# Weighing the kept sums of two experts on VectorE, and adding them by DMA, in a fused attention and mixture-of-experts kernel

## The chip, the cores and the metric

The kernel runs on one core of a Trainium2 chip. The metric is the time of one execution on the device, in microseconds (us), as the median of several runs. Lower is better. Engines are called PE (TensorE, the matrix engine), DVE (VectorE), ACT (ScalarE), POOL (GpSimd) and SP (SyncE, which here does nothing but issue transfers).

## The reference, cut to what matters

An attention block turns `q`, `k`, `v` into `x`, 4352 tokens of 128 features. Then a mixture of eight experts, with weights `P` for each token and expert that come from a balancing iteration, makes the output:

```
def _moe_ref(x, w_gate, w1, w2):            # x 4352 x 128, w1 8 x 128 x 1024, w2 8 x 1024 x 128
    P = np.exp(x @ w_gate - max)
    for _ in range(8):                      # rows, then columns, scaled to equal sums
        ...
    out = np.zeros((N, D))
    for e in range(8):
        ye = np.maximum(x @ w1[e], 0.0) @ w2[e]
        out += P[:, e:e + 1] * ye
    return out
```

Every expert is applied to every token. A weight `P[:, e]` is positive, so it may be multiplied onto a token's `x` ahead of the two products and the relu between them, or onto the expert's output behind them. All of it is float32.

## The kernel before

The features lie along the 128 partitions and the tokens along the columns (`xT`, 128 x 4352). `P` depends on all tokens, so the weights are ready only some way into the kernel. They lie in DRAM as `pT`, one row for each expert, and a row is read into SBUF as a broadcast over the partitions (`weights_of`, L788).

**Groups and items.** Work is cut into groups of tokens (`groups`, L713) and, within a group, into its experts; a group and an expert are an item. Groups 0 to 7 are done ahead of the weights: they apply expert 0 to all tokens and expert 1 to the first 1280. Their results stay in SBUF without a weight, as `kept[0]` (128 x 4352) and `kept[1]` (128 x 1280). From group 8 (`PLAIN`) on, `x` is multiplied by the weights first, so the products of all experts of a group can be summed in PSUM. Groups 8 to 12 have 768 tokens each, as three parts of 256 (`NT3`), starting at tokens 1280, 512, 2048, 2816 and 3584; they run experts 1 to 7, the one at 512 experts 2 to 7. The last group is the 512 tokens from 0, with experts 2 to 7.

**The middle stage.** These weighted groups of three parts are run by `middle()` (L1258). An item is two blocks; a block makes 128x384 first products (`x` times `w1`, PE, L1275), their relus and copies on ACT (L1301 to L1307), sums of them on DVE (L1312, L1177), and second products (the sums times sums of `w2`, PE, L1492). Both matrix products are done with fewer multiplications than the plain form has, which is what the sums on DVE are for: ten a block on L1177, four on L1312. The order of instructions on PE, DVE and ACT is written out by hand: `add(at, do)` enters a step at a due time, in a period of `PERIOD` = 8.83 us per block, and the steps are issued in order of these times. The due times only set the order; the engines run as soon as their semaphores allow. POOL and SP get their instructions in the order of the program too (`keep_in_program_order`). DVE, ACT, POOL and SP each run their queue in order, so an instruction that waits holds up all behind it.

**Spare slots.** Work that is not tied to a place, such as bringing the output together, goes into a list, `later`. `at_ease()` is called three times for each block (`EASE`) and issues one piece of `later` each time; pieces of `soon` are issued at once at the next call. `at_leisure(do)` puts a piece into `later` by way of `soon`.

**The input of an item.** `fetch_weights` (L815) loads the 768 weights of an item as `px`, on SP. `weigh_half` (L825, L832) multiplies `xT` by them on DVE, in two halves of 384 columns. The second half is wanted with a minus sign, so `negate` (L818, L823) makes a negated copy of that half of `xT` on ACT once per group. `copy_half` copies both halves on ACT, and `join_halves` (L843, L848) adds across halves and partitions with four accumulating DMAs on POOL's queue. The joined tiles `xe` and `de` feed PE.

**The kept sums.** `weigh_kept` (L853) brings the results of experts 0 and 1 into a weighted group. For each kept expert, it loads the weights of the group's tokens (`pb`) and multiplies `kept` by them, in pieces of 128x256, on POOL (`weigh`, L797): three pieces for each group of three parts, six for the group at 512 (where expert 1 is kept as well), four for the last group. Where expert 1 is kept, an accumulating DMA (`plus`) adds `kept[1]` to `kept[0]`; for the last group a subtraction on half of the partitions follows on POOL (`less`, L873). These steps are entered 5, 8.7, 12.4 and 16.1 us behind the start of an item near the beginning of the group (the third and later ones in `PLAIN`).

**The output of a group.** When a group's sums in PSUM are complete, `evacuate` and `part_of_twenty` (L990) copy them to SBUF and bring the four banks together in `y` (three parts of 128x256), with some twenty additions and subtractions on DVE (L999) through the spare slots. The last of these are three additions of the weighted `kept[0]` (L1039, L1040). Then `put` (L882) transposes each part on DVE (`yt`, L884) and stores it from SP (L1050), four or eight transfers for each.

Of the kernel before, what the change touches and what calls it, by code (L numbers as in the profile page):

```python
# [10 lines left out]
F32 = mybir.dt.float32  # L11
U32 = mybir.dt.uint32
Act = mybir.ActivationFunctionType
Alu = mybir.AluOpType
# [36 lines left out]
def kernel(  # L51
# [12 lines left out]
    nc = tc.nc  # L64
    P = nc.NUM_PARTITIONS
# [49 lines left out]
    own = consts.tile([P, H], F32, name="own")  # L115
# [9 lines left out]
    xT = big.tile([P, N + 2 * 32], F32, name="xT")  # L125
# [11 lines left out]
    pT = dram.tile([E, N], F32, name="pT")  # L137
# [14 lines left out]
    for i in range(2):  # L152
        t = wk.tile([P, H + 1, NT + 1, D], F32, name=f"v{i}", bufs=1)
# [3 lines left out]
    loaded, pools = {}, []  # L157
# [551 lines left out]
    NT3 = 256  # L709
# [6 lines left out]
    PLAIN = len(groups)  # L716
# [8 lines left out]
    kept = [keep.tile([P, N], F32, name="kept0"), keep.tile([P, 1280], F32, name="kept1")]  # L725
    items = [(g, e) for g, group in enumerate(groups) for e in group[3]]
# [59 lines left out]
        store_four(items[j][1], loaded_w[j][2])  # L786

    def weights_of(e, lo, n, tag):  # L788
        if tag == "pb":
            pb = spare[:, 6 * NT3 + 2 * HALF:9 * NT3 + 2 * HALF][:, 0:n]  # L790
        else:
            pb = pools[0].tile([P, 3 * NT3], F32, tag=tag, name=tag, bufs=3)[:, 0:n]
        tc.keep_in_program_order(nc.sync.dma_start(out=pb, in_=pT[e:e + 1, lo:lo + n].to_broadcast([P, n])))
        return pb

    def weigh(out, x, pb):
        tc.keep_in_program_order(nc.gpsimd.tensor_tensor(out, x, pb, op=Alu.mult))  # L797
# [12 lines left out]

    HALF = 3 * NT3 // 2
    spare = hb[:, 25 * NT3:]
    weights, turned_off = {}, {}

    def fetch_weights(j):  # L815
        weights[j] = weights_of(items[j][1], groups[items[j][0]][0], 3 * NT3, "px")

    def negate(g):  # L818

        lo = groups[g][0]  # L820
        c = 6 * NT3 + HALF * (g % 2)
        x = turned_off[g] = spare[:, c:c + HALF]
        nc.scalar.activation(out=x, in_=xT[:, lo + HALF:lo + 2 * HALF], func=Act.Copy, scale=-1.0)  # L823

    def weigh_half(j, i, engine):  # L825

        g = items[j][0]
        lo = groups[g][0]
        if i == 0:
            sources[j] = [pools[0].tile([P, 2, HALF], F32, tag="xe", name="xe", bufs=3)]  # L830
        x = turned_off[g] if i else xT[:, lo:lo + HALF]
        ins = engine.tensor_tensor(sources[j][0][:, i], x, weights[j][:, HALF * i:HALF * (i + 1)], op=Alu.mult)  # L832
        if engine is nc.gpsimd:
            tc.keep_in_program_order(ins)

    def copy_half(j, i):

# [12 lines left out]
    first_weighted = next(j for j, (g, e) in enumerate(items) if g == PLAIN)  # L850
    first_new = first_weighted + 2

    def weigh_kept(g, i):  # L853

        lo, n, t, es, _ = groups[g]
        ys = [kept[e][:, lo:lo + n * t] for e in range(es[0])]
        if i < len(ys):
            pb = []

            def piece(c):  # L860
                if not c:
                    pb.append(weights_of(i, lo, n * t, "pb"))
                sl = slice(c, c + NT3)
                weigh(ys[i][:, sl], ys[i][:, sl], pb[0][:, sl])

            return [lambda c=c: piece(c) for c in range(0, n * t, NT3)]

        def plus(y):
            tc.keep_in_program_order(nc.gpsimd.dma_start(out=ys[0], in_=y, accum_op=Alu.add))

        def less():
            k1, k2 = ys[0][upper, 0:n], ys[0][upper, n:2 * n]
            tc.keep_in_program_order(nc.gpsimd.tensor_tensor(k1, k1, k2, op=Alu.subtract))  # L873

        return [lambda y=y: plus(y) for y in ys[1:]] + [less] * (t == 2)

    def at_leisure(do):

        soon.append(lambda: later.append(do))
# [110 lines left out]
    def part_of_twenty(g, k):  # L990
# [7 lines left out]
        def do(out, a, b, off=False):  # L998
            at_leisure(lambda: nc.vector.tensor_tensor(out, a, b, op=Alu.subtract if off else Alu.add))  # L999

        if k == 0:
            own["y"] = pools[0].tile([P, 3, NT3], F32, tag="y", name="y")
            do(own["y"][:, 0], own[0][:, 0], own[0][:, 1])
        y = own["y"]
        if k == 1:
            do(y[:, 1], own[1][:, 0], own[0][:, 0], True)
        elif k == 2:
            do(y[upper, 2], own[2][upper, 0], own[0][upper, 0], True)
            do(y[lower, 2], own[2][lower, 0], own[0][lower, 1], True)
            do(y[lower, 2], y[lower, 2], own[2][lower, 1], True)  # L1010
            do(y[lower, 1], y[lower, 1], own[1][lower, 1], True)
        if all(i in own for i in range(4)):
            e0, e1, e2, e3 = (own[i] for i in range(4))
            t, c = (room(a).rearrange("p (s n) -> p s n", s=2) for a in "rx")
# [21 lines left out]
            do(y[:, 0], y[:, 0], c[:, 0])  # L1036
            do(y[upper, 2], y[upper, 2], t[upper, 1], True)
            do(y[lower, 2], y[lower, 2], d[lower], True)
            for i in range(3):  # L1039
                do(y[:, i], y[:, i], kept[0][:, lo + NT3 * i:lo + NT3 * (i + 1)])  # L1040
            for i in range(3):
                at_leisure(lambda i=i: put(y[:, i], lo + NT3 * i, NT3, (nc.sync,)))

# [214 lines left out]
    def middle():  # L1258
# [4 lines left out]
        def add(at_, do, *a):  # L1263
            jobs.append((at_, len(jobs), lambda: do(*a)))
# [98 lines left out]
        def at_ease():  # L1363
            while soon:
                soon.pop(0)()
            if later:
                later.pop(0)()

        for n, k in enumerate([ks[0] - 1] + ks, -1):
            if k == ks[-1] or items[blocks[k][0]][0] != items[blocks[k + 1][0]][0]:  # L1370
# [2 lines left out]
        for n, k in enumerate(ks):  # L1373
# [5 lines left out]
            if q == 0:  # L1379
# [17 lines left out]
                        add(t + at_, lambda: sums_ahead[j + 1].pop(0)())  # L1397
                late = 2 if g == PLAIN else 0
                if 1 + late <= es.index(e) <= es[0] + 1 + late:
                    for i, do in enumerate(weigh_kept(g, es.index(e) - 1 - late)):  # L1400
                        add(t + 5 + 3.7 * i, do)
                if g == len(groups) - 2 and 3 <= es.index(e) <= 5:
                    for i, do in enumerate(weigh_kept(len(groups) - 1, es.index(e) - 3)):
                        add(t + 5 + 3.7 * i, do)
            ahead = j + 2 + q
            if new_of(ahead):
                if q:
                    add(t + WEIGH - 9, fetch_weights, ahead)
                    if items[ahead - 1][0] != items[ahead][0]:
                        add(t + WEIGH, negate, items[ahead][0])  # L1410
                add(t + WEIGH, weigh_half, ahead, 1 - q, nc.vector)
                add(t + 13.69, copy_half, ahead, 1 - q)
                if not q:
                    add(t + WEIGH + 1, join_halves, ahead)
# [29 lines left out]
        for i, at_ in enumerate((10, 20.13, t + 15.43, t + 20.13, 2 * t + 15.43, 2 * t + 18, 2 * t + 28, 2 * t + 26,  # L1444
                                 3 * t + 20)):
            add(at_, lambda i=i: own[i]())
        add(WEIGH - 0.6, weigh_half, first_new + 2, 0, nc.vector)
        add(WEIGH - 0.2, copy_half, first_new + 2, 0)
        def begin_two(k):
            ready[k] = two(k)  # L1450
# [57 lines left out]
    def beside(j, c):  # L1508
# [17 lines left out]
        if new_of(j + 1) or new_of(j + 2):  # L1526
            for do, *a in PREPARE.get(c if new_of(j + 1) else c - 16, ()):
# [1 line left out]

    pieces, BESIDE = [], {}  # L1530

    PREPARE = {-14: ((fetch_weights, first_new),), -9: ((weigh_half, first_new, 0, nc.vector),),
               -8: ((negate, PLAIN), (copy_half, first_new, 0)), -7: ((weigh_half, first_new, 1, nc.vector),),
               -6: ((copy_half, first_new, 1),), -5: ((join_halves, first_new),),
               0: ((fetch_weights, first_new + 1), (raw_second, first_new, "ws"), (first_weights, first_new)),
               4: ((weigh_half, first_new + 1, 0, nc.vector),), 5: ((weigh_half, first_new + 1, 1, nc.vector),),
               6: ((copy_half, first_new + 1, 0),), 7: ((copy_half, first_new + 1, 1),),
               8: ((join_halves, first_new + 1),)}

# [191 lines left out]
```

## Time and profile before

| what | value |
|---|---|
| time, median of 3 runs | 892.82 us (892.56 to 892.99) |
| the profiled execution's own time, and its span | 892.21 us, 890.4 us |
| PE busy | 880.1 us (99% of the span) |
| DVE busy | 788.3 us (89%), 1595 instructions |
| ACT busy | 561.7 us (63%) |
| POOL busy | 180.9 us (20%), 242 instructions |
| mean granted TensorE clock | 0.999 |
| HBM traffic over the span | 167 GB/s |

The span is the stretch that the profiler's records cover; the execution's own time has 1.8 us around it. "Busy" counts an engine while it has an instruction under way. PE works as row tiles of 64x64, two or more at a time, so a busy PE may still have one of its tiles idle. In the views below, "L1177 DVE ... hb<-hb" is the instruction of line 1177 on DVE that writes tile `hb` and reads tile `hb`; "SPq" and "POOLq" are queues that issue transfers. In a row of the groups of instructions, the count is followed by the busy time in us and the mean of one in ns, then the idle time of the engine ahead of them and what ended it. A row of the timeline has its start, the stretch that it covers, and the number of instructions that it holds. A row of windows has the stretch and its length, and the busy time and number of instructions of PE, PEld (weight loads), DVE, ACT and POOL, then the granted clock, the DMA engines' busy share and GB/s.

### The profile page before, as it was taken

Reading aid. Unit: us, or ns where it says so; the run is one execution under the profiler, and the core shown is the slowest. Engines: PE = TensorE matmul, PEld = TensorE weight load, DVE = VectorE, ACT = ScalarE, POOL = GpSimd, SP = SyncE. Lnnn points to the kernel's source line nnn. Section 1 sums busy time; section 2 is a strip of 40 time slices with the busy share of each in tenths; the row PEclk is TensorE's granted clock in tenths of the full one; section 3 lists DMA queues with packets and bytes.
Section 4 is the critical chain, followed back from the end, with each engine's and each line's share of the span. In section 5 each row is a group of like instructions: output and inputs, shape, how many; then the busy total and the mean of one; then the engine's idle time right before and its main releaser. Section 6 shows DMA issues by size and latency. Waiting matters only on the chain.

```text
span 890.4 us, 28221 instructions
## 1 busy us (share of the span) xinstructions
PE 880.1 (99%) x11586; PEld 615.3 (69%) x11586; DVE 788.3 (89%) x1595; ACT 561.7 (63%) x1288; POOL 180.9 (20%) x242
## 2 busy tenths in 40 slices
PE   8999999999999999999999999999999999999997
PEld 6777544555677777676777777777777786666665
DVE  7678788889799999999999998999989999987865
ACT  3355477666577676676767666766667676655543
POOL 3121123012133213321222211321122213100000
PEclk9999999999999999999999999999999999999999
DMA  9996359658989777767776687567676775750340
GB/s 257 304 282 228 95 106 215 165 151 184 292 249 237 233 209 239 205 183 187 215 238 160 179 213 227 170 186 211 197 194 186 233 210 152 173 176 28 116 103 13
DMA packets 92721, 169.13 MB, mean 190 GB/s; under 512 B 28704, under 2 KB 65008, under 8 KB 87744
## 3 DMA queue, kind: packets, MB, share of 16 engines
q1 hardware_dynamic: 73264, 137.68, 49.2%
q0 software_dynamic: 18096, 29.49, 18.7%
q8 instruction: 91, 1.49, 0.7%
q10 hardware_dynamic: 1232, 0.16, 0.1%
q14 instruction: 38, 0.31, 0.1%
HBM read 123.60 MB, written 25.08 MB: 167 GB/s over the span
## 4 chain that ended last, share of the span: by engine, by line
PE 92%; DVE 5%; ACT 1%; issue 1%; DMA 1%; SPq 0%; DVEq 0%; ACTq 0%
PE s L1492 39%; PE a L1275 34%; PE a L1091 14%; PE a L423 1%; DVE hb L1177 1%; PE a L538 1%; DVE hx L1177 1%; DMA kx<-in_k_dram 1%; PE a L390 0%; DVE hb L1110 0%; PE s L452 0%; PE a L502 0%; DVE a L1312 0%; DVE hx L1312 0%; PE s L468 0%
## 5 line engine op out<-in xcount | busy, mean ns | idle before, releaser
L1275 PE MATMUL a<-xe,w 64*64 64x384 f32 x2052 | 397.4, 483 | 0.0
L1492 PE MATMUL s<-hb,ws 64*64 64x256 f32 (+4 forms) x2904 | 375.8, 384 | 1.6 <-DVE hb L1110 0.9
L1492 PE MATMUL s<-hx,ws 64*64 64x256 f32 (+1 forms) x2844 | 350.8, 377 | 0.4 <-DVE hx L1177 0.3
L1275 PE MATMUL a<-de,w 64*64 64x384 f32 x1536 | 299.2, 483 | 0.4 <-DVE a L1312 0.4
L1492 PEld LDWEIGHTS s<-hb,ws 64*64 64x64 f32 (+1 forms) x2904 | 197.0, 133 | 77.9 <-issue 30.8
L1492 PEld LDWEIGHTS s<-hx,ws 64*64 64x64 f32 (+1 forms) x2844 | 191.8, 133 | 60.9 <-issue 10.9
L1177 DVE TENSOR_TENSOR hb<-hb 128x512 f32<-128x512 f32 (+1 forms) x340 | 187.3, 576 | 3.6 <-ACT hb L1307 2.2
L1275 PEld LDWEIGHTS a<-xe,w 64*64 64x64 f32 x2052 | 139.9, 133 | 27.7 <-issue 0.9
L1307 ACT ACTIVATE hb<-a 128x384 f32<-128x384 f32 x192 | 91.5, 492 | 61.9 <-PE a L1275 57.1
L1307 ACT ACTIVATE hx<-a 128x384 f32<-128x384 f32 x192 | 91.0, 492 | 62.0 <-PE a L1275 59.2
L1177 DVE TENSOR_TENSOR hx<-hx 128x512 f32<-128x512 f32 (+1 forms) x204 | 122.9, 615 | 0.2
L1275 PEld LDWEIGHTS a<-de,w 64*64 64x64 f32 x1536 | 106.3, 133 | 22.3 <-DVE a L1312 1.5
L1091 PE MATMUL a<-xT,w 128*64 128x416 f32 (+3 forms) x512 | 119.2, 463 | 0.0
L1095 ACT ACTIVATE hb<-a 128x256 f32<-128x256 f32 (+4 forms) x152 | 68.8, 461 | 59.8 <-PE a L1091 54.0
L848 POOL DMA_DIRECT2D de<-xe x64 | 53.2, 975 | 226.2 <-PE a L1275 113.9
L1091 PE MATMUL a<-px,w 128*64 128x256 f32 (+1 forms) x512 | 93.1, 407 | 0.1
L1303 ACT ACTIVATE hb<-a 128x384 f32<-128x384 f32 x128 | 62.7, 490 | 32.5 <-PE a L1275 31.8
L1312 DVE TENSOR_TENSOR a<-a,hb 128x384 f32<-128x384 f32 x128 | 71.9, 562 | 7.3 <-PE a L1275 3.5
L1110 DVE TENSOR_TENSOR hb<-hb 128x416 f32<-128x416 f32 (+7 forms) x84 | 58.6, 698 | 21.2 <-ACT hb L1095 17.5
L1301 ACT COPY a<-a 128x384 f32<-128x384 f32 x128 | 59.3, 463 | 27.5 <-PE a L1275 26.6
L1095 ACT ACTIVATE hx<-a 128x256 f32<-128x256 f32 (+1 forms) x104 | 41.6, 400 | 42.8 <-PE a L1091 35.5
L1091 PEld LDWEIGHTS a<-xT,w 128*64 128x64 f32 x512 | 49.6, 137 | 24.6 <-issue 15.0
(217 smaller groups left out, 1034.9 us busy)
## 6 DMA issues: line engine op xcount, KB each, us to landing
ws<-ws SPq DMA_DIRECT2D x34, 1280.0 KB, 6.4
w<-wl SPq DMA_DIRECT2D x32, 512.0 KB, 8.4
w<-wf SPq DMA_DIRECT2D x32, 512.0 KB, 8.7
px<-pT SPq DMA_DIRECT2D x34, 384.0 KB, 9.3
w<-in_moe_w_dram SPq DMA_DIRECT2D x18, 512.0 KB, 4.2
de<-xe POOLq DMA_DIRECT2D x32, 192.0 KB, 3.5
de<-de POOLq DMA_DIRECT2D x32, 192.0 KB, 8.4
ph<-qa SPq DMA_DIRECT2D x12, 288.0 KB, 4.6
```

The source lines that it names most:

```text
L423: nc.tensor.matmul(pv[64 * s:64 * (s + 1), i], kp[0:n, H * t + h].rearrange("p i j -> p (i j)"), vx[0:n, slots[h], t, :], start=(t == 0 an ...
L848: tc.keep_in_program_order(nc.gpsimd.dma_start(out=out, in_=x, accum_op=Alu.add))
L1091: nc.tensor.matmul(ph[sl], loaded_w[j][0][:, P * f + H2 * s:P * f + H2 * (s + 1)], sources[j][:, lo:hi], start=True, stop=True, tile_posit ...
L1095: last_relu[:] = [nc.scalar.activation(out=out, in_=ph, func=Act.Relu).ins.name]
L1110: nc.vector.tensor_tensor(out, a, b, op=Alu.subtract)
L1177: nc.vector.tensor_tensor(places(out), places(a), places(b), op=Alu.subtract if off else Alu.add)
L1275: nc.tensor.matmul(out[sl], w[r, c0 + H2 * s:c0 + H2 * (s + 1)], x[r], start=start, stop=stop, tile_position=(H2 * row, H2 * s), skip_grou ...
L1301: witness(k, p, 1, nc.scalar.copy(b, bx))
L1303: witness(k, p, 5, nc.scalar.activation(out=m5s[p], in_=b, func=Act.Copy, scale=1.0 if p else -1.0))
L1307: ins = nc.scalar.activation(out=out, in_=x, func=Act.Relu)
L1312: ins = nc.vector.tensor_tensor(by if what == 1 else raw(k, p, 1, 1), bb[p], m5s[p], op=Alu.add)
L1492: mm = nc.tensor.matmul(sums[g][i][H2 * s:H2 * (s + 1), n * place:n * (place + 1)], w, x, start=c == (2 if t == 3 and row is None else 1) ...
```

## The change

The multiplications of `kept` by the weights move from POOL to DVE, with the same pieces of 128x256. They are entered 18 us behind the start of the same item, into a new list `urgent`, which `at_ease` serves ahead of `later`, so that each takes one of the spare slots. Their weights are loaded 5 us behind the start of the item, into a place of their own for each of two kept experts. The adding DMA of expert 1 (`plus`) is entered 12 us behind the start of its item, and the subtraction for the last group (`less`) goes to DVE, two blocks and 5 us behind.

The three additions of `kept[0]` to `y` on DVE are removed. In their place `add_kept` issues three accumulating DMAs on POOL's queue, one for each part of `y`, from one spare slot that stands behind the steps for bank 2 of the group, ahead of the rest of the additions into `y`.

`negate` is removed. The second half of an item's input is made by one `scalar_tensor_tensor` on DVE, `(xT * -1) * weights`, in place of the product with the negated copy.

```
@@ -786,10 +786,7 @@
         store_four(items[j][1], loaded_w[j][2])
 
     def weights_of(e, lo, n, tag):
-        if tag == "pb":
-            pb = spare[:, 6 * NT3 + 2 * HALF:9 * NT3 + 2 * HALF][:, 0:n]
-        else:
-            pb = pools[0].tile([P, 3 * NT3], F32, tag=tag, name=tag, bufs=3)[:, 0:n]
+        pb = pools[0].tile([P, 3 * NT3], F32, tag=tag, name=tag, bufs=3)[:, 0:n]
         tc.keep_in_program_order(nc.sync.dma_start(out=pb, in_=pT[e:e + 1, lo:lo + n].to_broadcast([P, n])))
         return pb
 
@@ -810,28 +807,23 @@
 
     HALF = 3 * NT3 // 2
     spare = hb[:, 25 * NT3:]
-    weights, turned_off = {}, {}
+    weights = {}
 
     def fetch_weights(j):
         weights[j] = weights_of(items[j][1], groups[items[j][0]][0], 3 * NT3, "px")
 
-    def negate(g):
-
-        lo = groups[g][0]
-        c = 6 * NT3 + HALF * (g % 2)
-        x = turned_off[g] = spare[:, c:c + HALF]
-        nc.scalar.activation(out=x, in_=xT[:, lo + HALF:lo + 2 * HALF], func=Act.Copy, scale=-1.0)
-
-    def weigh_half(j, i, engine):
+    def weigh_half(j, i):
 
         g = items[j][0]
         lo = groups[g][0]
         if i == 0:
             sources[j] = [pools[0].tile([P, 2, HALF], F32, tag="xe", name="xe", bufs=3)]
-        x = turned_off[g] if i else xT[:, lo:lo + HALF]
-        ins = engine.tensor_tensor(sources[j][0][:, i], x, weights[j][:, HALF * i:HALF * (i + 1)], op=Alu.mult)
-        if engine is nc.gpsimd:
-            tc.keep_in_program_order(ins)
+        sl = slice(HALF * i, HALF * (i + 1))
+        out, x, pb = sources[j][0][:, i], xT[:, lo:][:, sl], weights[j][:, sl]
+        if i:
+            nc.vector.scalar_tensor_tensor(out, x, -1.0, pb, op0=Alu.mult, op1=Alu.mult)
+        else:
+            nc.vector.tensor_tensor(out, x, pb, op=Alu.mult)
 
     def copy_half(j, i):
 
@@ -850,29 +842,37 @@
     first_weighted = next(j for j, (g, e) in enumerate(items) if g == PLAIN)
     first_new = first_weighted + 2
 
-    def weigh_kept(g, i):
+    urgent = []
+
+    def weigh_kept(g, i, at_, add):
 
         lo, n, t, es, _ = groups[g]
         ys = [kept[e][:, lo:lo + n * t] for e in range(es[0])]
-        if i < len(ys):
-            pb = []
-
-            def piece(c):
-                if not c:
-                    pb.append(weights_of(i, lo, n * t, "pb"))
-                sl = slice(c, c + NT3)
-                weigh(ys[i][:, sl], ys[i][:, sl], pb[0][:, sl])
-
-            return [lambda c=c: piece(c) for c in range(0, n * t, NT3)]
+        pb = spare[:, (6 + 3 * (i % 2)) * NT3:][:, 0:n * t]
+
+        def load():
+            tc.keep_in_program_order(nc.sync.dma_start(out=pb, in_=pT[i:i + 1, lo:lo + n * t].to_broadcast([P, n * t])))
+
+        def piece(c):
+            y = ys[i][:, c:c + NT3]
+            nc.vector.tensor_tensor(y, y, pb[:, c:c + NT3], op=Alu.mult)
 
         def plus(y):
             tc.keep_in_program_order(nc.gpsimd.dma_start(out=ys[0], in_=y, accum_op=Alu.add))
 
         def less():
             k1, k2 = ys[0][upper, 0:n], ys[0][upper, n:2 * n]
-            tc.keep_in_program_order(nc.gpsimd.tensor_tensor(k1, k1, k2, op=Alu.subtract))
-
-        return [lambda y=y: plus(y) for y in ys[1:]] + [less] * (t == 2)
+            nc.vector.tensor_tensor(k1, k1, k2, op=Alu.subtract)
+
+        if i < len(ys):
+            add(at_ + 5, load)
+            for c in range(0, n * t, NT3):
+                add(at_ + 18 + 1e-4 * c, urgent.append, lambda c=c: piece(c))
+        else:
+            for y in ys[1:]:
+                add(at_ + 12, plus, y)
+            if t == 2:
+                add(at_ + 2 * PERIOD + 5, less)
 
     def at_leisure(do):
 
@@ -998,6 +998,11 @@
         def do(out, a, b, off=False):
             at_leisure(lambda: nc.vector.tensor_tensor(out, a, b, op=Alu.subtract if off else Alu.add))
 
+        def add_kept():
+            for i in range(3):
+                tc.keep_in_program_order(nc.gpsimd.dma_start(
+                    out=own["y"][:, i], in_=kept[0][:, lo + NT3 * i:lo + NT3 * (i + 1)], accum_op=Alu.add))
+
         if k == 0:
             own["y"] = pools[0].tile([P, 3, NT3], F32, tag="y", name="y")
             do(own["y"][:, 0], own[0][:, 0], own[0][:, 1])
@@ -1009,6 +1014,7 @@
             do(y[lower, 2], own[2][lower, 0], own[0][lower, 1], True)
             do(y[lower, 2], y[lower, 2], own[2][lower, 1], True)
             do(y[lower, 1], y[lower, 1], own[1][lower, 1], True)
+            at_leisure(add_kept)
         if all(i in own for i in range(4)):
             e0, e1, e2, e3 = (own[i] for i in range(4))
             t, c = (room(a).rearrange("p (s n) -> p s n", s=2) for a in "rx")
@@ -1037,8 +1043,6 @@
             do(y[upper, 2], y[upper, 2], t[upper, 1], True)
             do(y[lower, 2], y[lower, 2], d[lower], True)
             for i in range(3):
-                do(y[:, i], y[:, i], kept[0][:, lo + NT3 * i:lo + NT3 * (i + 1)])
-            for i in range(3):
                 at_leisure(lambda i=i: put(y[:, i], lo + NT3 * i, NT3, (nc.sync,)))
 
     def store(yt, b0, b1, queues):
@@ -1363,8 +1367,8 @@
         def at_ease():
             while soon:
                 soon.pop(0)()
-            if later:
-                later.pop(0)()
+            if urgent or later:
+                (urgent or later).pop(0)()
 
         for n, k in enumerate([ks[0] - 1] + ks, -1):
             if k == ks[-1] or items[blocks[k][0]][0] != items[blocks[k + 1][0]][0]:
@@ -1397,18 +1401,14 @@
                         add(t + at_, lambda: sums_ahead[j + 1].pop(0)())
                 late = 2 if g == PLAIN else 0
                 if 1 + late <= es.index(e) <= es[0] + 1 + late:
-                    for i, do in enumerate(weigh_kept(g, es.index(e) - 1 - late)):
-                        add(t + 5 + 3.7 * i, do)
+                    weigh_kept(g, es.index(e) - 1 - late, t, add)
                 if g == len(groups) - 2 and 3 <= es.index(e) <= 5:
-                    for i, do in enumerate(weigh_kept(len(groups) - 1, es.index(e) - 3)):
-                        add(t + 5 + 3.7 * i, do)
+                    weigh_kept(len(groups) - 1, es.index(e) - 3, t, add)
             ahead = j + 2 + q
             if new_of(ahead):
                 if q:
                     add(t + WEIGH - 9, fetch_weights, ahead)
-                    if items[ahead - 1][0] != items[ahead][0]:
-                        add(t + WEIGH, negate, items[ahead][0])
-                add(t + WEIGH, weigh_half, ahead, 1 - q, nc.vector)
+                add(t + WEIGH, weigh_half, ahead, 1 - q)
                 add(t + 13.69, copy_half, ahead, 1 - q)
                 if not q:
                     add(t + WEIGH + 1, join_halves, ahead)
...
-    PREPARE = {-14: ((fetch_weights, first_new),), -9: ((weigh_half, first_new, 0, nc.vector),),
-               -8: ((negate, PLAIN), (copy_half, first_new, 0)), -7: ((weigh_half, first_new, 1, nc.vector),),
+    PREPARE = {-14: ((fetch_weights, first_new),), -9: ((weigh_half, first_new, 0),),
+               -8: ((copy_half, first_new, 0),), -7: ((weigh_half, first_new, 1),),
                -6: ((copy_half, first_new, 1),), -5: ((join_halves, first_new),),
                0: ((fetch_weights, first_new + 1), (raw_second, first_new, "ws"), (first_weights, first_new)),
-               4: ((weigh_half, first_new + 1, 0, nc.vector),), 5: ((weigh_half, first_new + 1, 1, nc.vector),),
+               4: ((weigh_half, first_new + 1, 0),), 5: ((weigh_half, first_new + 1, 1),),
                6: ((copy_half, first_new + 1, 0),), 7: ((copy_half, first_new + 1, 1),),
                8: ((join_halves, first_new + 1),)}
 
```

More of the change, by code (lines that the diff above doesn't have):

```diff
@@ L1446, in middle @@
             add(at_, lambda i=i: own[i]())
-        add(WEIGH - 0.6, weigh_half, first_new + 2, 0, nc.vector)
+        add(WEIGH - 0.6, weigh_half, first_new + 2, 0)
         add(WEIGH - 0.2, copy_half, first_new + 2, 0)
```

## The prediction

> **What bounds the kernel now.** I read the page first (span, busy shares, chain of work that ended last), then the timeline of SyncE as a clock of TensorE's progress, then the busy time of single blocks by windows, then VectorE's timeline in the blocks that stand out.
>
> ```profile
> span 890.4 us, 28221 instructions
> PE 880.1 (99%) x11586; PEld 615.3 (69%) x11586; DVE 788.3 (89%) x1595; ACT 561.7 (63%) x1288; POOL 180.9 (20%) x242
> PE 92%; DVE 5%; ACT 1%; issue 1%; DMA 1%; SPq 0%; DVEq 0%; ACTq 0%
> ```
>
> TensorE is busy for 99% of the span and carries 92% of the chain. VectorE work counts only where it makes TensorE late. A "99%" can hide that, because a waiting row tile is counted with its neighbour, so I need the length of the blocks themselves. In the middle stage one item (a group and an expert) is two blocks, and the load of its successor's `wl` is released by the same product of every item. The distances of these issues on SyncE are therefore the lengths of the items:
>
> ```profile
> 261.55 0.32 SPq L768 DMA_DIRECT2D w<-wl  x1
> ...
> 279.68 0.31 SPq L768 DMA_DIRECT2D w<-wl  x1
> ...
> 332.67 0.32 SPq L768 DMA_DIRECT2D w<-wl  x1
> ...
> 350.76 0.32 SPq L768 DMA_DIRECT2D w<-wl  x1
> ...
> 369.50 0.32 SPq L768 DMA_DIRECT2D w<-wl  x1
> ...
> 387.16 0.32 SPq L768 DMA_DIRECT2D w<-wl  x1
> ...
> 563.81 0.42 SPq L768 DMA_DIRECT2D w<-wl  x1
> ...
> 582.42 0.32 SPq L768 DMA_DIRECT2D w<-wl  x1
> ...
> 688.41 0.32 SPq L768 DMA_DIRECT2D w<-wl  x1
> ...
> 706.52 0.32 SPq L768 DMA_DIRECT2D w<-wl  x1
> ...
> 724.18 0.32 SPq L768 DMA_DIRECT2D w<-wl  x1
> ...
> 742.35 0.32 SPq L768 DMA_DIRECT2D w<-wl  x1
> ...
> 760.48 0.32 SPq L768 DMA_DIRECT2D w<-wl  x1
> ```
>
> An undisturbed item takes 387.16 - 369.50 = 17.66 us. Seven items are longer: 18.13, 18.09, 18.74, 18.61, 18.11, 18.17 and 18.13, that is 0.47 + 0.43 + 1.08 + 0.95 + 0.45 + 0.51 + 0.47 = 4.36 us too much. These are the items in which, or just after which, GpSimd multiplies kept sums (one multiplication of eight, near 452, costs nothing):
>
> ```profile
> L797 POOL TENSOR_TENSOR kept<-kept,hb 128x256 f32<-128x256 f32 x22 | 23.9, 1107 | 73.8 <-DMA hb<-pT 73.8
> L1177 DVE TENSOR_TENSOR hb<-hb 128x512 f32<-128x512 f32 x204 | 133.7, 681 | 3.4 <-ACT hb L1307 2.2 <-ACT hb L1095 0.7
> ```
>
> The first row is the group of those 22 multiplications, eight times two or three of them; the second VectorE's commonest sum, 0.68 us. Then the busy time of four single blocks, by windows:
>
> ```profile
> 261.02:270.32 9.30, 9.19 (x141) 6.36 (x136) 9.30 (x23) 6.51 (x17) 3.94 (x5) 1.00 0.94 251
> 448.45:457.28 8.83, 8.83 (x140) 6.34 (x136) 8.82 (x19) 5.80 (x14) 4.80 (x5) 1.00 0.29 99
> 572.11:581.88 9.77, 9.51 (x140) 6.69 (x136) 9.77 (x19) 5.83 (x14) 4.63 (x5) 1.00 0.44 107
> 617.23:626.06 8.83, 8.83 (x141) 6.76 (x136) 8.77 (x19) 5.80 (x14) 1.60 (x2) 1.00 1.01 307
> ```
>
> After the block's length come PE, PEld, DVE, ACT and POOL. With the same 19 instructions VectorE needs 8.77 us without GpSimd's multiplications and 9.77 us beside them (572.11). Its timeline shows which of its instructions stretch:
>
> ```profile
> 620.46 1.88 DVE L1177 TENSOR_TENSOR hb<-hb 128x512 f32<-128x512 f32 x3
> ...
> 575.16 1.19 DVE L1177 TENSOR_TENSOR hb<-hx 128x512 f32<-128x512 f32 x1
> 576.28 2.35 DVE L1177 TENSOR_TENSOR hx<-hx 128x512 f32<-128x512 f32 x2
> ...
> 452.07 1.82 DVE L1177 TENSOR_TENSOR hx<-hx 128x512 f32<-128x512 f32 x2
> ...
> 259.95 0.95 DVE L1177 TENSOR_TENSOR hb<-hx 128x256 f32<-128x256 f32 x1
> ```
>
> Three sums of 512 columns take 1.88 us undisturbed, 0.60 from start to start (0.68 alone, so 0.08 overlaps). Beside GpSimd's three multiplications the same three run from 575.16 to 576.28 + 2.35 = 578.63, 3.47 instead of 1.88: VectorE loses 1.6 us, TensorE 0.95. Near 452 two take 1.82 instead of 1.28: 0.54 lost, TensorE nothing. So TensorE absorbs some 0.65 us of VectorE's lateness, and the rest lengthens the block.
>
> **The change, part by part.** *GpSimd's 22 multiplications go.* With them goes all that I see stretching VectorE in the middle stage: -4.36 us.
>
> *VectorE gets 22 multiplications of 128x256 and one subtraction, and loses 15 additions.* Rows of the same shapes:
>
> ```profile
> L1177 DVE TENSOR_TENSOR hb<-hb 128x256 f32<-128x256 f32 x136 | 56.7, 417 | 0.2
> L999 DVE TENSOR_TENSOR y<-y,kept 128x256 f32<-128x256 f32 x15 | 6.1, 415 | 0.0
> L832 DVE TENSOR_TENSOR xe<-hb,px 128x384 f32<-128x384 f32 x32 | 18.0, 562 | 0.2
> L681 DVE SCALAR_TENSOR_TENSOR p<-rs,p 128x272 f32<-128x272 f32 x8 | 3.5, 442 | 0.3
> L823 ACT ACTIVATE hb<-xT 128x384 f32<-128x384 f32 x5 | 2.6, 517 | 0.0
> ```
>
> Each occupies 0.417 - 0.08 = 0.34 us, so the balance is +8 x 0.34 = 2.7 us of VectorE. They are not extra instructions in a full block: `at_ease` comes three times per block and takes one piece of `urgent` or `later`. The block at 617.23 has all three taken and still takes 8.83 us. So where a block only has the three, the cost on the path is zero, and its cover is TensorE's own 8.83 us; the cover is gone where a block holds more. That is group PLAIN, where `make_four` builds weights: the window 261.02 has 23 instructions, and VectorE is busy for all of it. There the three multiplications (3 x 0.34 = 1.0 us) come on top, where the stretched sum at 259.95 (0.95 instead of 0.42) had cost TensorE 0.47. Bounds: 0.3 us (0.65 absorbed) and 1.0 (nothing absorbed, since VectorE has no idle time to catch up). I take 0.75, nearer to the upper end, because 0.53 lost there cost 0.47. **+0.75 us.**
>
> *No negated copy.* ScalarE loses 5 copies of 0.52 us, at 63% load: nothing. VectorE's 32 products with that copy become scalar_tensor_tensor on `xT`. The row is 442 ns for 272 columns, beside 417 for 256: 25 ns for 16 columns more, where the sums give (681 - 417) / 256 = 1.03 ns per column, so 16 ns. So +10 ns each, 0.3 us in all, hidden; bounds -0.3 and +1 us. The Trainium skill (Vector Engine (DVE) Microarchitecture Reference, section "Points that are easy to get wrong") says that this form with two SBUF sources that are not bf16 runs at half throughput. The row L681 has two such sources and does not bear it out. By that rule the sum would be 891.0 (a rival below).
>
> *Three adding DMAs per group* go into GpSimd's queue ahead of a join (L848):
>
> ```profile
> 612.26 1.65 POOL L848 DMA_DIRECT2D de<-xe  x2 [11.13 <-PE a L1275]
> ...
> DMA to landing us min/median/max: 3.1/6.0/11.0
> ...
> 771.54 0.72 POOL L873 TENSOR_TENSOR kept<-kept 64x256 f32<-64x256 f32 x1 [9.59 <-DMA kept<-kept]
> ```
>
> Two issues take 1.65 us, three some 2.5, and GpSimd had been idle for 11.13 us before the join shown. The next VectorE step on `y` lies fifteen slots (five blocks, 44 us) later: hidden. A multiplication of kept sums waits only for its own load of `pT`. GpSimd waited 73.8 / 8 = 9.2 us for each of these; the planner now asks for it 15.8 us ahead (5 against 20.76): hidden. The subtraction for the last group moves to VectorE, where everything queues behind it. Its adding DMA needs 9.6 us (771.54), and the planner leaves 10.7 and the wait for a slot: zero, at worst about 1 us.
>
> *Stores move.* The removed and added slots shift the three transposes of a group, and SyncE issues in order: stores, then `ws`, `wl`, `wf`, `px`. In three groups of four the three transposes now fall into one block, the last at the late slot. For the group at 512 (eight stores for its third part) that delays the next `ws`:
>
> ```profile
> 517.94 0.44 DVE L884 STREAM_TRANSPOSE yt<-y 128x256 f32<-128x256 f32 x1
> ...
> 523.69 4.30 SPq L1050 DMA_DIRECT2D out_dram<-yt  x8
> 528.71 0.34 SPq L230 DMA_DIRECT2D ws<-ws  x1
> ...
> 539.08 0.38 PE L1492 MATMUL s<-hx,ws 64*64 64x256 f32 x2
> ...
> DMA to landing us min/median/max: 4.7/6.5/9.5
> ```
>
> The late slot is at 517.94 in the block before, so 8.83 later, 526.77; its transpose ends at 527.2, eight stores take 4.3, and `ws` is asked for at 531.5 instead of 528.71. It is first read at 539.08, 7.6 us later; the last row is the landing time of all `ws`. Median: in time. Longest: 1.9 us late. **+0.4 us**, bounds 0 and 1.9.
>
> Sum: -4.36 + 0.75 + 0.4 = -3.2 us. The profiled execution took 892.2 us (span 890.4 and 1.8 around it), which gives 889.0; the runs' median, 892.82, lies 0.6 above it: **889.6 us**.
>
> **Rivals.**
>
> *Adding DMAs delay the joins (slower).* An item's join has to land before its first block, and the three DMAs, 384 KB, go ahead of one join in each of four groups. The join asked for at 612.26 is for the item that begins one item after the block at 617.23, at 634.9, 22.6 us later; with the DMAs issued 2 us ahead there are some 24.8 us for 384 + 288 + 288 KB: below 39 GB/s TensorE waits. The slowest row, 256 KB in 9.6 us, is 27 GB/s if it had the queue to itself, but 288 KB of joins were ahead of it. At 35 GB/s the four joins are late by 2.6 us each: 889.6 + 10.4 = 900.0 us. Against it: the joins land in 6.0 us at the median (192 or 96 KB, queue included).
>
> *VectorE's length, not the stretch, made the blocks late (no change).* Then the moved work costs what the stretch did: 892.5 us. Against it stands the window 617.23, full and not late.
>
> *Half rate of scalar_tensor_tensor.* 384 x 1.03 ns = 0.40 us for each; the four in PLAIN's full blocks cost up to 1.6, elsewhere the 0.65 absorbs it: about +1.4, 891.0 us. Against it stands L681.
>
> *`ws` late by its longest landing*, there and in one more group: +1.5 to +2, 891.3 us.
>
> **How the numbers follow.** Forecast 0.72 (its own range 888.6 to 891.0: both bounds of 0.75 and most of those of 0.4, and 0.3 of spread between runs); joins 0.06; no change 0.08; half rate 0.06; late `ws` 0.08. This kernel's measurement can tell 0.2%, 1.8 us, from no change, so faster means below 891.03. All of the forecast, and half of the last two, are faster: 0.79. Same: the other halves and most of "no change" (0.06), 0.13. Slower: the joins and the rest of "no change", 0.08. The range 888.4 to 891.9 leaves out the joins, the no-change case and little else.
>
> **What would show it.** Items of 17.66 us at all seven places but the first; VectorE's 512-column sums at 0.68 everywhere in the stage; one or two long blocks between 261 and 280, together some 0.75 us; scalar_tensor_tensor near 0.57 us; `ws` asked for late once, near 528. Wrong would be: items longer than 17.66 in the blocks that now weigh, a TensorE wait for `de` or `xe` after the adding DMAs, or a VectorE wait for them.

## The result, and the profile after

The changed kernel takes 889.50 us (median of 7 runs, 888.18 to 890.28), the kernel before 892.82 us (median of 7, 890.98 to 893.26). The ratio is 0.9965, with a 95% interval of 0.9954 to 0.9977: faster by 0.35%. The forecast was 889.6 us. The profiled execution took 889.38 us, against a forecast of 889.0 for it.

The head of the page after, and its chain that ended last:

```profile
span 887.6 us, 28218 instructions
...
PE 876.5 (99%) x11586; PEld 627.7 (71%) x11586; DVE 783.7 (88%) x1603; ACT 559.6 (63%) x1283; POOL 169.6 (19%) x234
...
PE 91%; DVE 4%; DMA 3%; issue 1%; ACT 1%; SPq 0%; DVEq 0%; POOLq 0%; ACTq 0%
```

The shares barely move: TensorE stays at 99%, VectorE goes from 89% to 88%. What moved can be read only from the lengths of the items. SyncE's issues of `wl` in the changed kernel, at the places that were shown of before (start, duration, instruction):

```profile
262.05 0.32 SPq L768 DMA_DIRECT2D w<-wl  x1
...
280.43 0.32 SPq L768 DMA_DIRECT2D w<-wl  x1
...
333.42 0.32 SPq L768 DMA_DIRECT2D w<-wl  x1
...
351.09 0.32 SPq L768 DMA_DIRECT2D w<-wl  x1
...
368.75 0.32 SPq L768 DMA_DIRECT2D w<-wl  x1
...
386.41 0.32 SPq L768 DMA_DIRECT2D w<-wl  x1
...
563.05 0.32 SPq L768 DMA_DIRECT2D w<-wl  x1
...
580.71 0.32 SPq L768 DMA_DIRECT2D w<-wl  x1
...
686.69 0.48 SPq L768 DMA_DIRECT2D w<-wl  x1
...
704.36 0.32 SPq L768 DMA_DIRECT2D w<-wl  x1
...
722.02 0.32 SPq L768 DMA_DIRECT2D w<-wl  x1
...
739.83 0.32 SPq L768 DMA_DIRECT2D w<-wl  x1
...
757.55 0.32 SPq L768 DMA_DIRECT2D w<-wl  x1
```

Of the seven long items, four are clean now: 17.67, 17.66, 17.66 and 17.67 us. The first, in group `PLAIN`, takes 18.38 us, 0.72 more than a clean one, and the last two 17.81 and 17.72, 0.15 and 0.06 more. So 4.36 us of excess became 0.93, and the middle stage is 3.43 us shorter. The span is only 2.8 us shorter, because in this execution the middle stage began 0.5 us later than in the profile of before and the part behind it took 0.1 us more. In the profiles of the experiments below, the first product of that stage starts anywhere from 219.8 to 222.0 us, with nothing changed ahead of it. So I compare the stage by its blocks, and whole times by medians.

Windows of four blocks of the changed kernel (stretch and length, then busy time and count of PE, PEld, DVE, ACT and POOL, the clock, the DMA share, GB/s):

```profile
270.54:279.90 9.36, 9.12 (x141) 6.32 (x136) 9.36 (x23) 6.43 (x15) 1.65 (x2) 1.00 0.76 233
...
315.23:324.06 8.83, 8.83 (x141) 6.23 (x137) 7.72 (x16) 5.76 (x14) 1.72 (x2) 1.00 0.99 300
...
571.35:580.18 8.83, 8.83 (x140) 7.06 (x136) 8.29 (x18) 5.80 (x14) 3.40 (x4) 1.00 0.75 173
580.18:589.01 8.83, 8.83 (x140) 7.05 (x136) 8.64 (x19) 5.79 (x14) 1.74 (x2) 1.00 0.98 297
```

The third row is the block that took 9.77 us before (572.11). The fourth holds the three multiplications that VectorE now makes, and it is not longer. The first is the block in `PLAIN` where VectorE is busy for all of the time and TensorE waits.

### The profile page after: what moved, and what is told of

Same layout as the page of the kernel before. It is cut to its first block, busy times and chain, and to the rows that moved or that the text cites. A ratio compares the mean times of both kernels' runs of the same rounds, so it can differ in the third digit from the quotient of the medians.

```text
span 887.6 us, 28218 instructions
## 1 busy us (share of the span) xinstructions
PE 876.5 (99%) x11586; PEld 627.7 (71%) x11586; DVE 783.7 (88%) x1603; ACT 559.6 (63%) x1283; POOL 169.6 (19%) x234
## 3 DMA queue, kind: packets, MB, share of 16 engines
q8 instruction: 91, 1.49, 0.7%
## 4 chain that ended last, share of the span: by engine, by line
PE 91%; DVE 4%; DMA 3%; issue 1%; ACT 1%; SPq 0%; DVEq 0%; POOLq 0%; ACTq 0%
PE s L1492 39%; PE a L1279 34%; PE a L1095 13%; DMA ph<-in_moe_w_dram 1%; PE a L423 1%; DVE hb L1181 1%; DMA kp<-in_moe_w_dram 1%; PE a L538 1%; DMA kx<-in_k_dram 1%; PE a L390 0%; PE s L452 0%; DVE hx L1181 0%; DVE ws L244 0%; DVE hb L1114 0%; PE a L502 0%
## 5 line engine op out<-in xcount | busy, mean ns | idle before, releaser
L1492 PEld LDWEIGHTS s<-hb,ws 64*64 64x64 f32 (+1 forms) x2904 | 199.4, 134 | 76.1 <-issue 26.3
L1492 PEld LDWEIGHTS s<-hx,ws 64*64 64x64 f32 (+1 forms) x2844 | 195.3, 134 | 57.0 <-issue 11.9
L1181 DVE TENSOR_TENSOR hx<-hx 128x512 f32<-128x512 f32 (+1 forms) x204 | 118.3, 593 | 0.2
```

Source lines behind the costliest of these rows:

```text
L1181: nc.vector.tensor_tensor(places(out), places(a), places(b), op=Alu.subtract if off else Alu.add)
L1492: mm = nc.tensor.matmul(sums[g][i][H2 * s:H2 * (s + 1), n * place:n * (place + 1)], w, x, start=c == (2 if t == 3 and row is None else 1) ...
```

## The experiments

All times are medians. A kernel's profile is one execution of it. GpSimd's multiplications put back, the additions by VectorE, the unread halves and the unread copies ran beside each other (kernel before: 892.18 us), as did the other four (kernel before: 892.36 us). Each ratio is to the kernel before that ran beside it. The changed kernel itself was not run again, so differences of a few tenths from its 889.50 us are read from blocks and not from times.

**GpSimd multiplies the kept sums again** (the rest of the change stays):

```
-            for c in range(0, n * t, NT3):
-                add(at_ + 18 + 1e-4 * c, urgent.append, lambda c=c: piece(c))
...
+                    for i, do in enumerate(weigh_kept(g, es.index(e) - 1 - late)):
+                        add(t + 5 + 3.7 * i, do)
```

> The changed kernel with the other part undone: GpSimd multiplies the kept sums again, at the places and with the loads of the kernel before; the adding DMAs and the scalar_tensor_tensor products stay. Theory (GpSimd's multiplications stretch VectorE): the long blocks come back, 0.4 to 1.1 us each at seven places, and the time is that of the kernel before, 892.8 us within 0.7. Rival (the lighter VectorE work of the changed kernel made the difference): 889.5 to 890.5 us.

Measured: 892.86 us, ratio to before 1.0006 (0.9997 to 1.0015). All of the gain is gone, so it hung on who multiplies. Its profiled execution, 894.58 us, holds 2.3 us of another cause as well (a late `px`, below); taking them off leaves some 892.3 us, still the time of the kernel before. The issues of `wl` in its profile:

```profile
332.47 0.32 SPq L768 DMA_DIRECT2D w<-wl  x1
...
351.42 0.32 SPq L768 DMA_DIRECT2D w<-wl  x1
...
370.09 0.32 SPq L768 DMA_DIRECT2D w<-wl  x1
```

18.95 and 18.67 us stand where the changed kernel has 17.67 and 17.66.

**The additions to the outputs by VectorE again** (the adding DMAs are gone, GpSimd's multiplications too):

```
-            at_leisure(add_kept)
...
+            for i in range(3):
+                do(y[:, i], y[:, i], kept[0][:, lo + NT3 * i:lo + NT3 * (i + 1)])
```

> The changed kernel with one part undone: the three additions of the kept sums to a group's outputs are VectorE additions in spare slots again, and the adding DMAs are gone. Theory (the gain comes only from GpSimd's multiplications being gone; extra VectorE work in spare slots is free): as the changed kernel, 889.5 us within 0.5, and the same 0.7 us of long blocks in group PLAIN only. Rival (what counts is how much work VectorE has, 15 x 0.34 = 5.1 us of it back): up to 5 us of it returns, 892 to 894 us.

Measured: 888.38 us, ratio 0.9959 (0.9947 to 0.9972). With 15 more instructions than the changed kernel on VectorE, one more block is long by over 0.1 us: the one at 545 us, which takes 9.13 instead of 8.83. SyncE and VectorE there:

```profile
533.04 9.03 SPq L1055 DMA_DIRECT2D out_dram<-yt  x12
542.12 0.45 SPq L790 DMA_DIRECT2D px<-pT  x1
...
547.08 0.56 DVE L826 TENSOR_TENSOR xe<-xT,px 128x384 f32<-128x384 f32 x1 [1.56 <-PE a L1280]
```

The additions shift the stores of a group, and here twelve of them stand ahead of the load of `px`, which the changed kernel asks for at 532.94. The trace has this `px` landing at 546.96, and the product that reads it starts 0.12 us later. The row puts the wait down to TensorE; the landing is the nearer cause. So the block is late by the order of transfers, and not by a full VectorE, which has 7.53 us of work in it. The rival, by which VectorE's load sets the time, is out: 5.1 us of VectorE work cost at most 0.3 us. This also says what the adding DMAs bring by themselves: next to nothing.

**Products on GpSimd that nobody reads, in halves.** Into the changed kernel, beside the loads:

```
+        def idle(c0):
+            n2 = NT3 // 2
+            scrap = spare[:, 12 * NT3:12 * NT3 + n2]
+            for c in (c0, c0 + n2):
+                tc.keep_in_program_order(nc.gpsimd.tensor_tensor(
+                    scrap, xT[:, lo + c:lo + c + n2], pb[:, c:c + n2], op=Alu.mult))
...
+            for m, c in enumerate(range(0, n * t, NT3)):
+                add(at_ + 5 + 3.7 * m, idle, c)
```

> The changed kernel, with products on GpSimd added whose results nobody reads: for each 128x256 piece of the kept sums two products of 128x128, of x and the loaded weights, into a scratch place, asked for where the kernel before multiplied the pieces. Nothing waits for them. Theory (a GpSimd product with two SBUF inputs holds up VectorE's sums with two SBUF inputs): VectorE's 512-column sums beside them take about 1.2 us instead of 0.68, the blocks of the kernel before are long again, and the time is 889.5 + 3.5 to 4.5 = 893 to 894 us. Rival (what made blocks late before was a wait for the multiplied sums or their loads, not the GpSimd work): 889.5 us.

Measured: 890.46 us, ratio 0.9984 (0.9972 to 0.9997). Right in kind and wrong in size: its blocks lost 1.4 us against the changed kernel's, not 3.5 to 4.5. **Whole ones of 128x256**, at four of the eight places, test whether the size of one product is the reason:

```
+            scrap = kept[1][:, 512:512 + NT3]
+            tc.keep_in_program_order(nc.gpsimd.tensor_tensor(
+                scrap, xT[:, lo + c:lo + c + NT3], pb[:, c:c + NT3], op=Alu.mult))
...
+                if g >= PLAIN + 2 and i == 0:
+                    add(at_ + 5 + 3.7 * m, idle, c)
```

> The changed kernel with GpSimd products added whose results nobody reads, now of the 128x256 size of the removed multiplications, but only where a scratch place of that size is free: from the third weighted group on (four of the eight places: near 452, 572, 697 and 735 us). Theory (it is the size of one GpSimd product that sets how long VectorE is held, so that halves of 128x128 cost TensorE little and whole ones the old amount): the blocks of the kernel before at these places are long again, by about 0, 0.9, 0.45 and 0.3 us; 889.5 + 1.7 = 891.2 us. Rival (the size does not matter, the earlier multiplications held something else up): 0.2 us as with the halves, 889.7 us.

Measured: 889.87 us, ratio 0.9974 (0.9965 to 0.9984), 1.8 us above the 888.10 of a kernel with the changed kernel's blocks that ran beside it (the adds issued twice, below); the expectation had 1.7. The time alone lies nearer to the rival's 889.7, which was counted from 889.50, so the blocks have to decide. In its profile, that of the slowest of its ten executions (892.26 us), four blocks are long, by 0.45, 1.06, 0.46 and 0.48 us, of which the last has 0.15 in the changed kernel too: 2.3 us at four places, where the halves cost 1.4 at eight. The expectation had 0, 0.9, 0.45 and 0.3, so it missed the first. VectorE and GpSimd in the second of these, from its timelines:

```profile
575.61 1.26 DVE L1188 TENSOR_TENSOR hb<-hx 128x512 f32<-128x512 f32 x1
576.79 2.35 DVE L1188 TENSOR_TENSOR hx<-hx 128x512 f32<-128x512 f32 x2
...
575.59 2.99 POOL L869 TENSOR_TENSOR kept<-xT,hb 128x256 f32<-128x256 f32 x3 [10.27 <-DMA hb<-pT]
```

and the same place with halves, and with nothing (the changed kernel):

```profile
574.34 0.91 DVE L1189 TENSOR_TENSOR hb<-hx 128x512 f32<-128x512 f32 x1
575.17 1.80 DVE L1189 TENSOR_TENSOR hx<-hx 128x512 f32<-128x512 f32 x2
...
579.03 0.68 DVE L1189 TENSOR_TENSOR hb<-hx 128x256 f32<-128x256 f32 x1
...
574.25 5.18 POOL L871 TENSOR_TENSOR hb<-xT,hb 128x128 f32<-128x128 f32 x6 [10.28 <-DMA hb<-pT]
```

```profile
574.47 0.68 DVE L1181 TENSOR_TENSOR hb<-hx 128x512 f32<-128x512 f32 x1
575.07 1.28 DVE L1181 TENSOR_TENSOR hx<-hx 128x512 f32<-128x512 f32 x2
```

The same three sums end 1.88, 2.63 and 3.53 us after their start with nothing, halves and whole products beside them. Nobody waits for these products, so it is GpSimd's work itself that stretches VectorE. The halves go on for longer and stretch a fourth sum, at 579.03, by 0.26 us (0.42 without them). The block with the halves and then the block with the whole ones, by windows:

```profile
571.20:580.24 9.04, 9.04 (x140) 7.08 (x136) 8.69 (x17) 5.91 (x14) 5.60 (x8) 1.00 0.24 86
...
572.50:582.39 9.89, 9.51 (x140) 6.98 (x136) 9.54 (x18) 5.89 (x14) 6.64 (x8) 1.00 0.45 111
```

So the halves cost VectorE 0.75 + 0.26 = 1.0 us here and TensorE 0.2; the whole ones 1.65 and 1.06. TensorE absorbs 0.6 of the whole ones and 0.8 of the halves, which are spread over a longer stretch.

**Copies on GpSimd that nobody reads**, with `nc.gpsimd.tensor_copy(scrap, pb[:, c:c + n2])` in place of the half product, so one SBUF input:

> As the kernel with unread GpSimd products, but each of them is a copy of the loaded weights with one SBUF input. Theory (it takes GpSimd's reading of SBUF of any kind): VectorE's sums are stretched while a copy runs, in proportion to the copies' time; 890.5 to 894 us. Rival (only a GpSimd instruction with two inputs holds VectorE up): 889.5 us within 0.5 and 0.68 us for every 512-column sum.

Measured: 888.83 us, ratio 0.9974 (0.9960 to 0.9989). Same place:

```profile
573.86 0.68 DVE L1189 TENSOR_TENSOR hb<-hx 128x512 f32<-128x512 f32 x1
574.46 1.49 DVE L1189 TENSOR_TENSOR hx<-hx 128x512 f32<-128x512 f32 x2
...
574.42 3.14 POOL L871 COPY hb<-hb 128x128 f32<-128x128 f32 x6 [10.82 <-DMA hb<-pT]
```

Over 3.14 us of copies VectorE loses 0.21 us, and TensorE nothing; of all its blocks one is longer for them, by 0.2 us. Neither text fits quite: copies do stretch VectorE, against the rival, but by some 0.1 us a sum instead of "in proportion". The Trainium skill (SBUF — State Buffer, section "Who interferes with whom") says that a VectorE instruction with two SBUF inputs contends with a GpSimd instruction that reads SBUF. The trace agrees for products (three sums in 3.53 us instead of 1.88); for copies the effect is there (1.49 us instead of 1.28) and too small to matter here.

**The multiplications in `PLAIN` six blocks later**, on the changed kernel:

```
-                add(at_ + 18 + 1e-4 * c, urgent.append, lambda c=c: piece(c))
+                add(at_ + (70.98 if g == PLAIN else 18) + 1e-4 * c, urgent.append, lambda c=c: piece(c))
```

> The changed kernel with one due time changed: in group PLAIN the three multiplications of the kept sums on VectorE are asked for six blocks later, so that they fall behind that group's weight-making, into the block whose VectorE had 1.1 us free. Theory (in a block in which VectorE has no idle time each added instruction lengthens the block): the two long blocks, 9.02 and 9.36 us, become 8.83 and the time is 0.7 us shorter than that of the changed kernel, 888.8 us. Rival (those two blocks are late because of the start of the middle stage, as the 12.86 us of its first): they stay, 889.5 us.

Measured: 887.63 us, ratio to before 0.9948 (0.9935 to 0.9962). This is the fastest version. Windows of the two long blocks and of the block that took the work over:

```profile
260.26:269.09 8.83, 8.83 (x141) 7.19 (x136) 8.74 (x20) 6.41 (x16) 2.70 (x3) 1.00 0.85 220
269.09:277.92 8.83, 8.83 (x141) 7.12 (x136) 8.83 (x22) 6.43 (x14) 1.65 (x2) 1.00 0.83 247
...
313.24:322.07 8.83, 8.83 (x140) 7.23 (x136) 8.64 (x19) 5.80 (x13) 1.73 (x2) 1.00 0.99 307
```

9.02 and 9.36 became 8.83 twice, and the block with 16 VectorE instructions carries 19 at no cost. So three instructions of 0.34 us cost 0.72 us in one place and nothing six blocks on. Beside this run, the two kernels below, which have the changed kernel's blocks, took 888.02 and 888.10 us: in time the move brings 0.4 to 0.5 us (0.6 over the whole stage by its first and last products), which the runs can hardly tell from nothing, and it is the blocks that show it.

**The adding DMAs twice and three times** (`for i in (0, 1, 2) * 3`, and `* 2`); the kept sums are then added several times over:

> The changed kernel with its three adding DMAs issued three times, so that the kept sums are added three times over: nine transfers of 128 KB ahead of a join. Theory, worked out from the run with GpSimd's multiplications put back, where 672 KB of queued adds and joins took 12.5 us (54 KB/us): eight of the nine and the first half of the join, 1.3 MB, land some 24 us behind their issue, the second half 4 to 9 us later, and the join is 3 to 6 us late for its item in four or five groups: 902 to 918 us. Rival (the joins have far more room than that, or the adds do not share the queue's rate): 889.5 us.

> The changed kernel with its three adding DMAs issued twice (the kept sums are added twice over). Theory (a join has some 6 us of room, and three more transfers of 128 KB at 54 KB/us with the halves behind them use it up but not more): 889.5 to 891 us, joins landing one to three us ahead of their item. Rival (no room beyond what the changed kernel uses): 895 us or more.

Measured: 888.02 us for three times (two executions) and 888.10 us for twice (three), no block longer in either than in the changed kernel. The expectation for three times missed by 14 us or more. GpSimd's queue in the profile with nine adds, and then in the changed kernel:

```profile
572.66 2.61 POOL L1003 DMA_DIRECT2D y<-kept  x3 [8.90 <-DVE hx L1181]
...
579.02 2.64 POOL L1003 DMA_DIRECT2D y<-kept  x3 [1.57 <-DMA y<-kept]
581.11 2.26 POOL L840 DMA_DIRECT2D de<-xe  x2
592.69 0.88 POOL L840 DMA_DIRECT2D de<-de  x1 [9.33 <-DMA de<-xe]
```

```profile
563.45 1.55 POOL L1003 DMA_DIRECT2D y<-kept  x1
573.14 1.74 POOL L1003 DMA_DIRECT2D y<-kept  x2 [8.14 <-DVE y L999]
575.22 1.66 POOL L840 DMA_DIRECT2D de<-xe  x2 [0.34 <-ACT de L833]
580.81 0.88 POOL L840 DMA_DIRECT2D de<-de  x1 [3.93 <-DMA de<-xe]
```

With nine adds the join is asked for 5.9 us later and its second half 11.9 us later, at 592.69; counted from the blocks, which run 1.4 us earlier in this profile, 7.3 and 13.3 us late. The trace has its last piece landing at 596.83, 0.4 us behind the start of the item that it feeds, and that is still in time. From 572.66 to that landing are 24.2 us, where I had worked with 28 to 33. The rate under load was not the error: the last three adds and the two first halves, 672 KB from 579.02, landed by 592.16, which is 51 KB/us beside my 54. But the five adds ahead of them, 640 KB from 572.66, had landed by 580.28, at 84 KB/us, and the second half had landed 4.7 us behind the first, the low end of my 4 to 9; its two transfers took 3.0 and 3.6 us. In the changed kernel they take 7.7 and 9.7 us, from 580.81, when SyncE has just asked for `wl`, `wf` and `px`; with nine adds they come some 12 us behind these loads, and the DMA engines move 82 GB/s instead of 281. No run takes the loads away, so that they make the difference is likely and not shown.

With six adds the last piece lands at 590.94, 5.5 us ahead of its item, where its expectation had one to three. The room of a join is larger than I took it for, and the changed kernel uses none of it: in all four groups the join waits for ScalarE's copy alone.

## Why the prediction was right, point by point

*GpSimd's multiplications, -4.36 us.* The mechanism is shown from both sides: putting them back returns the whole time, and putting unread ones in makes blocks long at the same places. The term was 0.2 too large: the last two long items keep 0.15 and 0.06 us with GpSimd's multiplications gone. What keeps them was not followed; in the block with the 0.15, from 730.32, VectorE has only 7.78 us of work, and none of it on `kept`. The 0.65 us of VectorE's lateness that TensorE was to absorb came out as 0.6 to 0.8 beside the unread products.

*VectorE's 22 multiplications.* Free wherever a block has its three pieces of spare work, as the window 580.18 shows. In `PLAIN` they cost 0.72 us (18.38 - 17.66) where 0.75 was forecast; moving them shows that they are the cause. The forecast took this size from a loss of 0.53 us that had cost 0.47, but two sums just ahead, at 258.14 and 259.28, took 0.75 us instead of 0.68, so VectorE had lost 0.67 there. Worked out from that, the size would still be 0.7 to 0.8. None of the 22 waits for its weights (idle 0.0 in the first row). The rows of the moved and the new instructions:

```profile
L858 DVE TENSOR_TENSOR kept<-kept,hb 128x256 f32<-128x256 f32 x22 | 9.2, 416 | 0.0
...
L826 DVE TENSOR_TENSOR xe<-xT,px 128x384 f32<-128x384 f32 x32 | 17.8, 556 | 5.6 <-PE a L1279 4.8
...
L824 DVE SCALAR_TENSOR_TENSOR xe<-xT,px 128x384 f32<-128x384 f32 x32 | 17.5, 546 | 0.1
```

*scalar_tensor_tensor.* 546 ns, beside 556 for the plain product of the same size. The rival of half rate is out: it asked for some 400 ns more.

*`ws` late, +0.4.* This term failed; it is 0. The order that it rests on came as forecast: `ws` was asked for at 531.25 (531.5 forecast, 528.71 before), behind twelve stores:

```profile
522.71 8.44 SPq L1054 DMA_DIRECT2D out_dram<-yt  x12
531.25 0.68 SPq L230 DMA_DIRECT2D ws<-ws  x1
```

No block near there is over 8.83 us. I had weighed in a landing time longer than the median; the trace does not record this one's landing, so by how much it was in time is open. That stores ahead of a load can cost something shows the profile of the kernel with GpSimd's multiplications put back:

```profile
645.33 6.70 SPq L1051 DMA_DIRECT2D out_dram<-yt  x8
652.08 0.45 SPq L793 DMA_DIRECT2D px<-pT  x1
...
657.96 0.56 DVE L829 TENSOR_TENSOR xe<-xT,px 128x384 f32<-128x384 f32 x1 [3.56 <-DMA px<-pT]
```

There eight stores went ahead of `px`, VectorE waited 3.56 us for it, and that block took 11.10 us. The additions by VectorE had a milder case at 545 us. So the prediction looked at the right queue and at the wrong load: it was `px` that stores made late, in two of the variants and not in the changed kernel. The row of 3.56 us is from a single execution, the slowest of that kernel, 1.7 us above its median; in the changed kernel `px` is asked for at 647.50 and nothing waits.

*Adding DMAs.* Hidden, as forecast, but not as I described it. I had them issued 2 us ahead of a join with GpSimd idle. In fact the first goes out right behind the join before it, the second waits 8.14 us for VectorE's last step on `y`, and GpSimd's queue waits with it; the join then finds it free with 0.34 us to spare. The other three groups look the same: 6.0 to 8.6 us of waiting, 0.29 to 0.44 to spare. The prediction did not see this wait. The rival that made the joins late falls with the runs above: nine transfers instead of three lengthen no block. (Its 24.8 us should read 24.6, 22.6 + 2; nothing hangs on it.)

*Sum.* -4.15 (4.36 - 0.21) + 0.72 + 0 = -3.43 us in the blocks, -3.2 forecast; the two misses, 0.2 and 0.4, partly cancel. The medians moved by 3.3 us. That 889.6 and 889.50 agree to 0.1 us is luck: besides the two misses, the middle stage starts up to 2 us earlier or later from one execution to the next, and two kernels with the changed kernel's blocks took 888.0 and 888.1 us on another occasion.

## What to carry to other kernels

GpSimd arithmetic with two inputs beside a VectorE that has little room is not free, even if nobody waits for its result: look for VectorE instructions that take longer than the mean of their form, and see what GpSimd runs at that moment. A busy share cannot show it, since the stretched instruction counts as busy; lengths of equal blocks can. An instruction added to a full engine should be placed by the idle time of the single block, not by the mean: the same three cost 0.72 us or nothing.

## What the runs showed of the hardware

The size of one GpSimd product matters beyond its share of the work. At the same place three products of 128x256 stretched VectorE's sums by 1.65 us, six of 128x128 by 1.0 us in all, although GpSimd was busy longer with the six (5.18 us against 2.99). Copies with one input, 3.14 us of them, stretched by 0.21 us. The accumulating transfers of GpSimd's queue moved 84 KB/us at first and 51 KB/us at the end when nine adds and a join followed each other; in the changed kernel the two adds of 128 KB from 573.14 landed in 3.1 and 3.2 us. The second half of a join landed in 3.0 to 3.6 us when it came 6 us or more behind SyncE's loads of weights (the adds twice and three times), and in 7.7 to 9.7 us beside them.
